# A banded attention with a feed-forward network on one core: places of all work, zeros on TensorE, and signs of the weights on other engines

## The chip, the cores and the metric

The kernel runs on one core of a Trainium2 chip. The metric is the device time of one execution in microseconds, as the median of three runs. Of the core's engines the text uses these names: PE (TensorE, matrix products), DVE (VectorE), ACT (ScalarE), POOL (GpSimd), and SP (SyncE), whose queue starts DMAs. Each engine carries out its own instructions in the order in which they stand in the program; an instruction that waits for another engine holds up what stands behind it on its own.

## The reference

```python
scores = scale * np.matmul(q, k.transpose(0, 1, 3, 2))            # B, H, S, D = 4, 8, 768, 64
is_global = pos[None, :] < int(n_global)                          # 8
is_local = (rel >= 0) & (rel < int(n_local))                      # 96
keep = is_global | is_local
dist = np.where(is_global & ~is_local, float(n_local), np.abs(rel))
scores = np.where(keep, scores - slopes[:, None, None] * dist, -1e9)
a = np.exp(scores - np.max(scores, axis=-1, keepdims=True))
x = np.matmul(a / (np.sum(a, axis=-1, keepdims=True) + 1e-09), v)
h = x.reshape(3072, 512) @ w_in                                   # w_in 512 x 2048, float64
g = np.where(h >= 1, h, np.where(h <= -1, 0.0, (h + 1) ** 2 / 4))
return g @ w_out                                                  # w_out 2048 x 512, float64
```

(Cut and joined from two functions.) The result has 3072 rows of 512 floats.

## The kernel before

**Units and chunks.** The 3072 rows are 24 units of 128 rows (batch and block of rows). Each unit's attention is done in two halves of four heads. Two units make a chunk of 256 rows for the feed-forward network, so there are 12 chunks. Units 0 to 3, the first blocks of the four batches, need only their own block of keys and are computed in float32 (functions first_*). The other 20 are computed with float16 pairs: each operand is split into a high and a low half, and three products replace one.

**A half of the attention**, for units 4 to 23: scores on PE (L742), bias and row extreme on DVE (masked, L566), the exponential on ACT (L578), high half of the probabilities on ACT (L758) and low half on DVE (L760), a DMA transpose on SP's queue (turn_p, L767, tile pt), the product with the values on PE (L785, tile av), scaling on DVE (L627, tile x), high half on ACT (L799) and low half on POOL (L801, tile xh), and a second DMA transpose on SP's queue (turn_x, L809, tile xt). In the first four units PE does the transposes (L601 for the probabilities, tile tp; L641 for the result, tile xtp), ACT copies tp to pt (L608), and DVE splits xtp (L651).

**A chunk of the feed-forward network**: eight groups of ffn1 (L870: 24 matmuls into one PSUM tile h of 128x512, for two of the 16 blocks of the hidden width), each followed by the gelu steps: ACT (L883, tile u), two on DVE (L888, L893; the second releases h), ACT (L897, tile gh), POOL (L901, tile gl). Then for each of 16 blocks and each of the chunk's two row tiles t a triple of matmuls into the tile o (ffn2, L913). ACT scales the finished o into ob (L927), and SP's queue writes it out (L928). There are two PSUM buffers for h and two for o. The transposes tp of the first units also take an h buffer.

**The weights** come as float64. In 32 pieces (n = 0 to 15 of w_in, 16 to 31 of w_out) they are loaded as pairs of 32-bit words into three raw buffers (L454, SP) and turned into float32 by DVE in three steps on 128x512: w_bits step 0 takes exponent and mantissa from the upper word (L468), step 1 the sign (L472), step 2 adds the lower word (L475) and so releases the raw buffer. Then follow w_hi (ACT, L488), w_scale (ACT, L495) and w_lo (POOL, L502). The weights are loaded a second time in 64 half pieces through the same raw buffers to be checked for their range (check_load, L529, on SP; check_reduce, L534, on DVE, two reductions to a load). At the end DVE gathers all checks, POOL reduces them over the partitions, and the verdict (badi, L297, read at L298 on SP and the other engines) decides whether a general path has to run; with these inputs it does not.

**Zeros.** warm (L434) multiplies a tile of zeros by itself, 128x128 by 128x512, into a tile named spare that nobody reads (a spare o buffer). Before, there are 8 such matmuls at the start and 3 behind each of chunk 0's eight groups, 32 in all.

**What sets the order.** Every step is entered in a list by at(time, function, arguments), with planned times from the constants at the top of the file. The list is sorted by these times, and then the table PLACE says in which order its entries are emitted. The order of each engine's instructions, and of SP's DMAs, is that of PLACE; a step that is emitted early waits on its engine.

Of the kernel before, what the change touches and what calls it, by code (L numbers as in the profile page):

```python
# [10 lines left out]
F32 = mybir.dt.float32  # L11
# [6 lines left out]
P = 128  # L18
# [38 lines left out]
XL = "p"  # L57
# [6 lines left out]
FLOAD = [-0.95, -0.52, 15.64, 24.01]  # L64
VLOAD = [-4.77, 11.54, 18.15, 28.68]
FIRST = [4.37, 7.29, 10.29, 15.54, 26.68, 37.85, 48.2, 54.41]
WARM = [(1.0, 8)]
WLOAD = [0.8, 1.0, 8.0]
WA = 3
# [3 lines left out]
TAB = -0.77  # L73
TBC = -1.99
RC = 52.97
E3 = [-19.46, -14.0, -6.17, -0.47, 3.78, 8.46, 16.26, 20.67]
PER = 47.0
SOFF = -13.94
FETCH = 16.26
CONV = 9.6  # L80
KG = 3.41
CHK = 7.39
VCONV = 10.53
VFETCH = 8.71
AVL = 14.35
GEL = [2.7, 3.48, 4.59, 5.91, 5.91]
CK0 = 199.09
CK1 = 573.64
CKL = 10.36
WO = [2.79, 3.98, 5.09]  # L90
FO = [0.26, 1.06, 2.5, 3.37, 3.48, 4.67, 5.72, 6.5, 6.59, 7.54]
UO = [0.55, 1.5, 4.0, 5.66, 6.33, 1.69, 1.96, 3.06, 3.38, 3.41]
BO = [1.94, 2.51]
SO = [0.63, 0.65, 2.38, 1.0]
WS = "d"
RO = 0.18
W0 = 6.0
PA = 2.76
WG = 3.75
PB = 2.64  # L100
NCH = NU // 2
WLAG = 5.0
PLACE = [
# [208 lines left out]
def fast_path(ctx, tc, q, k, v, nraw, nval, w_in, w_out, out, half, nm, sums, sq, su):  # L312
# [119 lines left out]
    def warm(n):  # L432
        for _ in range(n):
            nc.tensor.matmul(  # L434
                spare(0).rearrange("p (a b) -> p a b", a=4), zeros, zeros.unsqueeze(1).to_broadcast([P, 4, P]),
                start=True, stop=True,
            )

    def piece(n):
# [756 lines left out]
```

## Time and profile before

| quantity | value |
|---|---|
| median of three runs | 638.66 us (638.55 to 640.11) |
| the profiled execution's own time | 637.52 us |
| its span, first to last instruction | 635.7 us |
| mean granted clock of PE | 0.980 |
| busy PE, DVE, ACT, POOL | 607.6, 442.2, 412.1, 296.8 us |
| zero matmuls (L434) | 32 |
| DVE steps L468, L472, L475 | 32 each |

The profile describes one execution. A row of a stage gives the stage's length, each engine's busy time with its number of instructions, and the granted clock of PE as a share of full speed. A row of the waits gives the engine, the line that waited, the engine, tile and line that released it, and then the total in us, the number of waits and the longest. A row of the timeline gives start, duration, engine, line, operation and tiles, and in brackets the idle time before it with its releaser. Engines overlap, so the shares of busy time do not add up, and a wait costs time only on the engine that is the limit at that moment.

### The profile page before, as it was taken

The page shows a single profiled execution, that of the slowest core. Times are in us where ns is not written, and L with a number is a line of the kernel's source. Part 1 is how long each engine was busy: PE and PEld are TensorE (multiplying, and loading weights), DVE is VectorE, ACT ScalarE, POOL GpSimd, SP SyncE. Part 2 cuts the span into 40 slices and gives each one's busy share as a digit, 9 for nine tenths or more (in the row PEclk, how much of TensorE's full clock was granted, in tenths as well). Part 3 has the DMA queues.
Part 4 walks back from the last instruction along what each step waited for, and adds up shares of the span by engine and source line. Part 5 has one row for each costly group of instructions (what it writes and reads, how often), then busy time and mean ns, then how long its engine had stood idle before and what let it go on. Part 6 is the DMA issues. An engine that isn't in the chain of part 4 may idle for free.

```text
span 635.7 us, 14747 instructions
## 1 busy us (share of the span) xinstructions
PE 607.6 (96%) x5588; PEld 417.1 (66%) x5588; DVE 442.2 (70%) x1109; ACT 412.1 (65%) x1070; POOL 296.8 (47%) x266
## 2 busy tenths in 40 slices
PE   7888799999999999999999999999999999999996
PEld 4666575656876766767767667666666766766652
DVE  6999999977956676776776776776677686533420
ACT  4868898998867665775785775676585674432220
POOL 0336785775563543563653563463554533322210
PEclk8889899999999999999999999999999999999999
DMA  6748586578944565556555555766554643531001
GB/s 201 250 147 247 182 252 197 125 134 191 168 93 75 109 154 141 154 146 163 144 139 135 158 135 144 171 143 139 127 165 110 140 133 78 125 116 35 1 34 39
DMA packets 144084, 88.08 MB, mean 139 GB/s; under 512 B 108165, under 2 KB 124549, under 8 KB 144005
## 3 DMA queue, kind: packets, MB, share of 16 engines
q1 hardware_dynamic: 144000, 87.05, 54.1%
q8 instruction: 46, 0.75, 0.5%
q14 instruction: 34, 0.27, 0.1%
q10 hardware_dynamic: 4, 0.00, 0.0%
HBM read 54.53 MB, written 6.29 MB: 96 GB/s over the span
## 4 chain that ended last, share of the span: by engine, by line
issue 31%; POOL 26%; PE 25%; DVE 9%; ACT 5%; DMA 2%; POOLq 0%; SPq 0%; ACTq 0%; DVEq 0%
PE o L913 13%; POOL gl L901 11%; PE h L870 8%; POOL xh L801 8%; POOL kh L698 2%; POOL kr L697 2%; DVE w_f L475 2%; POOL qh L698 2%; ACT z L578 1%; POOL qr L697 1%; DMA w_raw<-in_moe_w_out_dram 1%; PE av L785 1%; POOL wol L502 1%; DVE u L893 1%; PE s L742 1%
## 5 line engine op out<-in xcount | busy, mean ns | idle before, releaser
L870 PE MATMUL h<-xt,wih 128*128 128x256 f16 x1536 | 259.7, 274 | 0.7 <-DVE u L893 0.7
L901 POOL TENSOR_TENSOR gl<-u,gh 128x512 f16<-128x512 f32 x96 | 117.8, 1227 | 214.2 <-ACT gh L897 205.2
L870 PE MATMUL h<-xt,wil 128*128 128x256 f16 x768 | 210.8, 274 | 0.0
L870 PEld LDWEIGHTS <-wih 128*128 128x128 f16 x1536 | 149.4, 99 | 32.2 <-DVE u L893 1.6
L888 DVE SCALAR_TENSOR_TENSOR h<-h,u 128x512 f32<-128x512 f32 x96 | 66.7, 695 | 116.3 <-ACT u L883 115.5
L913 PE MATMUL o<-wol,gh 128*128 128x512 f16 x384 | 145.9, 380 | 1.7 <-POOL wol L502 1.7
L913 PE MATMUL o<-woh,gh 128*128 128x512 f16 x384 | 146.4, 381 | 0.0
L913 PE MATMUL o<-woh,gl 128*128 128x512 f16 x384 | 145.8, 380 | 0.0
L883 ACT ACTIVATE u<-h,half 128x512 f32<-128x512 f32 x96 | 65.4, 682 | 87.8 <-PE h L870 87.8
L913 PEld LDWEIGHTS <-gh 128*128 128x128 f16 x768 | 71.5, 98 | 67.2 <-issue 0.5
L578 ACT ACTIVATE z<-z,nm 128x256 f32<-128x256 f32 (+1 forms) x192 | 91.8, 479 | 28.0 <-DVE nm L566 27.5
L897 ACT ACTIVATE gh<-u 128x512 f16<-128x512 f32 x96 | 59.8, 623 | 51.1 <-DVE u L893 51.1
L566 DVE CUSTOM_DVE_ANT_0 z<-s,bias 128x256 f32<-128x256 f32 (+1 forms) x192 | 67.1, 397 | 22.2 <-PE s L742 20.4
L870 PEld LDWEIGHTS <-wil 128*128 128x128 f16 x768 | 75.6, 98 | 9.1
L913 PEld LDWEIGHTS <-gl 128*128 128x128 f16 x384 | 37.7, 98 | 47.7 <-issue 2.9
L760 DVE SCALAR_TENSOR_TENSOR ph<-z,ph 128x1024 f16<-128x1024 f32 x40 | 61.6, 1540 | 9.6 <-ACT ph L758 9.4
L801 POOL TENSOR_TENSOR xh<-x,xh 128x256 f16<-128x256 f32 x40 | 62.2, 1554 | 10.4 <-ACT xh L799 8.8
L893 DVE SCALAR_TENSOR_TENSOR u<-u,h 128x512 f32<-128x512 f32 x96 | 65.4, 681 | 1.4
L534 DVE TENSOR_REDUCE sq<-c_raw 128x1 f32<-128x256 f32 x128 | 49.1, 409 | 0.0
L785 PEld LDWEIGHTS <-pt 128*128 128x128 f16 x960 | 32.8, 98 | 14.5 <-DMA pt<-ph 7.1
L758 ACT ACTIVATE ph<-z 128x1024 f16<-128x1024 f32 x40 | 41.7, 1043 | 0.1
L785 PE MATMUL av<-vh,pt 128*128 128x64 f16 x960 | 34.6, 193 | 4.5 <-DMA pt<-ph 4.3
(100 smaller groups left out, 671.8 us busy)
## 6 DMA issues: line engine op xcount, KB each, us to landing
w_raw<-in_moe_w_in_dram SPq DMA_DIRECT2D x16, 512.0 KB, 4.0
w_raw<-in_moe_w_out_dram SPq DMA_DIRECT2D x16, 512.0 KB, 3.8
c_raw<-in_moe_w_in_dram SPq DMA_DIRECT2D x32, 256.0 KB, 3.5
c_raw<-in_moe_w_out_dram SPq DMA_DIRECT2D x32, 256.0 KB, 3.3
vr<-in_v_dram SPq DMA_DIRECT2D x28, 256.0 KB, 3.9
kr<-in_k_dram SPq DMA_DIRECT2D x28, 256.0 KB, 3.6
qr<-in_q_dram SPq DMA_DIRECT2D x24, 256.0 KB, 4.3
out_dram<-ob SPq DMA_DIRECT2D x24, 256.0 KB, 2.8
```

Of the source, the lines that this page charges most:

```text
L566: nc.vector.tensor_tensor_reduce(out=p32[u, hf][:, hh, :], in0=pts[u, hf][hh // 2][:, hh % 2, 0:n], in1=bias[:, 4 * hf + hh, base : base + n],
L578: nc.scalar.activation(z, z, AF.Exp, bias=nm[:, c : c + 1], scale=-1.0, accum_out=sums[:, c : c + 1])
L760: nc.vector.scalar_tensor_tensor(phs[u, hf][:, 1, :], zf, SP_, phs[u, hf][:, 0, :], op0=ALU.mult, op1=ALU.subtract)
L785: nc.tensor.matmul(av[:, hh, :], pt[:, a, hh, kt, :], vt[:, c, h * D : (h + 1) * D], start=(n == 0), stop=(n == 5),)
L801: (nc.gpsimd if XL == "p" else nc.vector).tensor_sub(xhs[u, hf][:, 1, :], xs[u, hf], xhs[u, hf][:, 0, :])
L870: nc.tensor.matmul(hp[:, e, :], w[:, dc, f], xt[:, hf, 2 * a + j, :], start=(n == 0), stop=(n == 3 * NDC - 1),)
L883: nc.scalar.activation(us[c, g], hs[c, g], AF.Relu, bias=half, scale=2.0 / (SV * SW), accum_out=su[:, col : col + 1])
L888: nc.vector.scalar_tensor_tensor(ws[c, g], hs[c, g], 4.0 / (SV * SW), us[c, g], op0=ALU.mult, op1=ALU.max)
L893: nc.vector.scalar_tensor_tensor(dst, us[c, g], 4.0, ws[c, g], op0=ALU.min, op1=ALU.mult)
L897: nc.scalar.activation(gh, ws[c, g], AF.Copy)
L901: (nc.gpsimd if GL == "p" else nc.vector).tensor_sub(gl, ws[c, g], gt[c, g][0])
L913: nc.tensor.matmul(po, a[:, cs], w[:, f, :], start=(f == 0 and n == 0), stop=(f == NFC - 1 and n == 2))
```

## The change

Lines of the changed file are 9 to 17 higher than those of before (L472 becomes L484, L475 L487, L893 L908, L801 L816, L913 L928, and so on). The change has these parts:

- **PLACE and all planned times** are new, so every engine's order is.
- **Signs.** WS was "d" (DVE for all pieces). Now every third piece (n = 2, 5, ..., 29; ten pieces) is marked "s": DVE leaves step 1 out. ACT takes the sign of the upper word in the raw buffer, in place (L482), and POOL multiplies the finished float32 piece by it (w_sign, L494), ahead of w_hi. In these pieces POOL and not DVE is the last reader of the raw buffer.
- **XL** was "p" and is "v": the low half of x (40 subtractions of 128x256) goes from POOL to DVE (L816).
- **Zeros.** The 8 at the start are gone (WARM), two instead of three stand behind each of the eight groups (WA), and 150 entries filler() of one zero matmul each are put in the list, of which PLACE uses 95. That makes 111 zero matmuls, all ahead of the first o matmul on PE: between the score, tp, av and xtp steps of the first units and behind the first h groups, in runs of 1 to 11.
- **Check loads**: their planned times were spread from 199 to 574 us and are now from 301 to 596. The reductions of the last three check loads now follow the last gelu step on DVE.
- **The end** (TAIL): the last chunk does all 16 triples of t = 0 and then all of t = 1, in place of both in turn. The last 128 rows are scaled in two halves of 256 columns, the first by ACT and the second by DVE, which waits for ACT's write to the same tile. The first half is written out by SP's queue, the second by ACT's.
- TPO = 0 leaves the two new branches on TPO without effect.

```diff
-XL = "p"
+XL = "v"
...
-WARM = [(1.0, 8)]
+WARM = []
...
-WA = 3
+WA = 2
...
-CK0 = 199.09
-CK1 = 573.64
-CKL = 10.36
...
+CK0 = 301.36
+CK1 = 595.7
+CKL = 10.95
...
-WS = "d"
...
+WS = 'ddsddsddsddsddsddsddsddsddsddsdd'
...
 PLACE = [
-    5, 0, 1, 2, 11, 3, 6, 4, 7, 9, 12, 38, 68, 20, 8, 10, 13, 151, 14, 15, 16, 17, 18, 19, 21, 22, 25, 23, 24,
...
+    3, 0, 1, 2, 5, 7, 9, 72, 10, 4, 73, 12, 74, 75, 36, 6, 76, 230, 77, 8, 11, 14, 15, 19, 16, 17, 13, 18, 20,
...
+NFILL = 150
+TAIL = 1
+TPO = 0
...
+    def filler():
+        warm(1)
...
-            if num < NFC and num % 2:
+            if num < NFC and num % 2 and not TPO:
...
-        tp = ps_h.tile([P, 4, P], F32, tag="h", name=f"tp{u}_{hf}")
+        if TPO and u >= TPO:
+            tp = spare(1).rearrange("p (a b) -> p a b", a=4)
+        else:
+            tp = ps_h.tile([P, 4, P], F32, tag="h", name=f"tp{u}_{hf}")
...
-            nc.scalar.activation(ob[:, cs], os_[c, t][:, cs], AF.Copy, scale=1.0 / (SG * SW))
-        nc.sync.dma_start(out[r0 : r0 + P, :], ob)
+            if e:
+                nc.vector.tensor_scalar(ob[:, cs], os_[c, t][:, cs], 1.0 / (SG * SW), None, op0=ALU.mult)
+            else:
+                nc.scalar.activation(ob[:, cs], os_[c, t][:, cs], AF.Copy, scale=1.0 / (SG * SW))
+        for e in range(parts):
+            cs = slice(e * n, (e + 1) * n)
+            (nc.scalar if e else nc.sync).dma_start(out[r0 : r0 + P, cs], ob[:, cs])
...
-                at(t + 0.2, finish, c, x, 1)
+                at(t + 0.2, finish, c, x, 2 if TAIL and c + 1 == NCH and x else 1)
...
-            put_ffn2(c, (0, 1), g, t - (PER / 16 - 0.1 if g and c + 1 < NCH else 0.0))
+            if TAIL and c + 1 == NCH:
+                put_ffn2(c, (0,), g, t0 + 1.3 * g)
+                put_ffn2(c, (1,), g, t0 + 10.5 + 1.3 * g)
+            else:
+                put_ffn2(c, (0, 1), g, t - (PER / 16 - 0.1 if g and c + 1 < NCH else 0.0))
...
+    for n in range(NFILL):
+        at(12.0, filler)
```

**DVE around the gelu step of chunk 0's group 5.** The tile h0_5 is that group's PSUM tile, whose buffer the last transpose tp of the first attention takes next; w16, w17 and w18 are pieces of the weights. Before, DVE's order reads:

```order
L468 TENSOR_SCALAR w17_bits_880<-w17_raw_803 128x512
L472 SCALAR_TENSOR_TENSOR w17_bits_880<-w17_raw_803,w17_bits_880 128x512
L888 SCALAR_TENSOR_TENSOR h0_5_823<-h0_5_823,u0_5_888 128x512
L651 TENSOR_TENSOR xt1_635<-xtp3_0_883,xt1_635 128x2x128
L893 SCALAR_TENSOR_TENSOR u0_5_888<-u0_5_888,h0_5_823 128x512
L475 SCALAR_TENSOR_TENSOR w17_f32_931<-w17_raw_803,w17_bits_880 128x512
L468 TENSOR_SCALAR w18_bits_941<-w18_raw_818 128x512
L472 SCALAR_TENSOR_TENSOR w18_bits_941<-w18_raw_818,w18_bits_941 128x512
```

After:

```order
L903 SCALAR_TENSOR_TENSOR h0_5_892<-h0_5_892,u0_5_939 128x512
L666 TENSOR_TENSOR xt1_658<-xtp3_0_936,xt1_658 128x2x128
L487 SCALAR_TENSOR_TENSOR w16_f32_974<-w16_raw_829,w16_bits_920 128x512
L480 TENSOR_SCALAR w17_bits_980<-w17_raw_882 128x512
L908 SCALAR_TENSOR_TENSOR u0_5_939<-u0_5_939,h0_5_892 128x512
L487 SCALAR_TENSOR_TENSOR w17_f32_992<-w17_raw_882,w17_bits_980 128x512
L480 TENSOR_SCALAR w18_bits_1000<-w18_raw_922 128x512
L484 SCALAR_TENSOR_TENSOR w18_bits_1000<-w18_raw_922,w18_bits_1000 128x512
L487 SCALAR_TENSOR_TENSOR w18_f32_1023<-w18_raw_922,w18_bits_1000 128x512
```

Piece 17 is one of the ten: its sign step (L472 before, L484 after) no longer stands between its first and its last step, and steps of pieces 16 and 17 stand at other places around the two gelu steps.

**SP's queue at the probabilities of unit 16.** xt7 is the transposed result of units 14 and 15, pt16_0 the transposed probabilities of unit 16's first half, c13_0, c5_1 and c6_0 are check loads, ob5 the output of chunk 5. Before:

```order
L676 DMA qr18_5_5420<-in_q_dram 128x512
L529 DMA c13_0_raw_5536<-in_moe_w_in_dram 128x2x256
L809 DMA_TRANSPOSE xt7_5014<-xh15_1_5538 128x4x128
L767 DMA_TRANSPOSE pt16_0_5555<-ph16_0_5529 128x16x128
L928 DMA out_0_dram<-ob5_0_5565 128x512
L928 DMA out_0_dram<-ob5_1_5594 128x512
```

After:

```order
L541 DMA c5_1_raw_5499<-in_moe_w_in_dram 128x2x256
L948 DMA out_0_dram<-ob5_0_5505 128x512
L948 DMA out_0_dram<-ob5_1_5541 128x512
L541 DMA c6_0_raw_5572<-in_moe_w_in_dram 128x2x256
L782 DMA_TRANSPOSE pt16_0_5633<-ph16_0_5609 128x16x128
L824 DMA_TRANSPOSE xt7_5023<-xh15_1_5626 128x4x128
```

The transpose pt16_0 stood behind that of xh15_1 and stands ahead of it now; the outputs of chunk 5 went ahead of both, and the check loads are of earlier pieces. At units 18 and 20 pt still stands behind an xt.

More of the change, by code (lines that the diff above doesn't have):

```diff
@@ L62 @@
 FQ = {"k": "sync", "q": "sync", "v": "sync"}
-FLOAD = [-0.95, -0.52, 15.64, 24.01]
-VLOAD = [-4.77, 11.54, 18.15, 28.68]
-FIRST = [4.37, 7.29, 10.29, 15.54, 26.68, 37.85, 48.2, 54.41]
-WARM = [(1.0, 8)]
+FLOAD = [-1.58, 1.06, 14.93, 25.91]
+VLOAD = [-7.73, 13.43, 17.25, 33.34]
+FIRST = [4.37, 6.86, 10.29, 15.54, 27.12, 37.85, 47.39, 54.41]
+WARM = []
 WLOAD = [0.8, 1.0, 8.0]
-WA = 3
+WA = 2
 T0 = 24.5
@@ L72 @@
 GB = 5.42
[L73 to L76, printed above, removed]
+TAB = -1.61
+TBC = -0.92
+RC = 61.5
+E3 = [-19.46, -14.0, -9.93, -2.34, 1.91, 6.59, 13.05, 20.27]
 PER = 47.0
[L78 to L86, printed above, removed]
-CK0 = 199.09
-CK1 = 573.64
-CKL = 10.36
[L90 to L94, printed above, removed]
-WS = "d"
-RO = 0.18
+SOFF = -3.14
+FETCH = 17.57
+CONV = 8.38
+KG = 0.88
+CHK = 5.61
+VCONV = 8.11
+VFETCH = 5.66
+AVL = 12.92
+GEL = [2.85, 3.46, 3.99, 6.47, 7.12]
+CK0 = 301.36
+CK1 = 595.7
+CKL = 10.95
+WO = [2.78, 4.07, 6.1]
+FO = [0.65, 1.06, 2.46, 3.92, 3.63, 4.69, 5.48, 6.56, 6.65, 6.93]
+UO = [0.55, 1.5, 3.54, 5.66, 7.51, 2.65, 3.43, 3.67, 3.99, 4.75]
+BO = [1.14, 2.16]
+SO = [0.58, 0.29, 3.06, 1.83]
+WS = 'ddsddsddsddsddsddsddsddsddsddsdd'
+RO = 0.28
 W0 = 6.0
 PA = 2.76
-WG = 3.75
-PB = 2.64
+WG = 4.92
+PB = 2.85
 NCH = NU // 2
-WLAG = 5.0
+WLAG = 6.05
 PLACE = [
[139 rows of a table removed]
-]
[145 rows of a table added]
+]
+NFILL = 150
+TAIL = 1
+TPO = 0
 @with_exitstack
```

282 rows, old and new, of the table PLACE are left out of this document.

## The prediction, on record before the changed kernel ran

> **What bounds the kernel now.** I read the clock first (one core, 0.980, span 635.7 us), then busy time by stage, then TensorE's waits, then the stretch of the trace around each wait. The stages:
>
> ```profile
> 10.00:72.00 62.00, 51.52 (x343) 39.55 (x343) 57.85 (x164) 49.05 (x139) 28.88 (x26) 0.83 0.63 199
> 72.00:125.00 53.00, 50.47 (x415) 34.38 (x416) 51.44 (x102) 48.64 (x116) 37.70 (x35) 0.97 0.65 185
> 125.00:220.00 95.00, 94.55 (x1043) 66.03 (x1041) 66.73 (x167) 74.83 (x202) 54.15 (x51) 1.00 0.68 135
> 220.00:609.00 389.00, 384.69 (x3676) 265.33 (x3674) 257.37 (x631) 235.42 (x610) 174.26 (x149) 1.00 0.51 128
> 609.00:629.50 20.50, 20.46 (x95) 9.09 (x93) 2.59 (x6) 1.84 (x4) 1.53 (x2) 1.00 0.01 3
> 629.50:635.70 6.20, 0.00 (x0) 0.00 (x0) 0.00 (x0) 0.60 (x2) 0.00 (x0) 0.92 0.26 91
> ```
>
> The columns are the stretch, its length, busy PE, PEld, DVE, ACT, POOL, granted clock, DMA share, GB/s. From 72 us on PE is busy 50.47 of 53, 94.55 of 95, 384.69 of 389: nothing but PE work or PE waits can be removed there. Up to 72 us PE idles 10.48 us, although zero matmuls fill part of it, while DVE is busy 57.85 of 62: DVE sets the pace of the start. What PE waits for, over 10 to 130 us and then to the end:
>
> ```profile
> PE tp L601 <- DVE u L893: 4.4, 2, 3.9
> PE o L913 <- POOL wol L502: 1.7, 2, 1.3
> PE h L870 <- DVE u L893: 0.5, 2, 0.3
> ...
> PE av L785 <- DMA pt<-ph: 4.3, 5, 1.4
> ```
>
> The 3.9 us are the last transpose of the first attention. It waits until DVE has worked through its list to the gelu step whose PSUM buffer it takes:
>
> ```profile
> 72.26 1.09 PE L601 MATMUL tp<-ident,z 128*128 128x128 f32 x4 [3.87 <-DVE u L893]
> 73.14 0.63 PE L913 MATMUL o<-woh,gh 128*128 128x512 f16 x1
> ...
> 75.35 1.00 PE L619 MATMUL av<-vr,pt 128*128 128x64 f32 x8
> 76.19 0.38 PE L913 MATMUL o<-woh,gh 128*128 128x512 f16 x1
> 76.40 0.38 PE L913 MATMUL o<-wol,gh 128*128 128x512 f16 x1
> ...
> 76.87 0.44 PE L641 MATMUL xtp<-ident,x 128*128 128x128 f32 x2
> 77.15 0.38 PE L913 MATMUL o<-woh,gh 128*128 128x512 f16 x1
> ...
> 77.80 0.38 PE L870 MATMUL h<-xt,wih 128*128 128x256 f16 x2
> ```
>
> Before the h at 77.80 (chunk 0's eighth group) stand all of the first attention and four o triples. An o matmul takes 0.21 us at the full clock (76.19 to 76.40), so a triple 0.65.
>
> **Part by part. Signs off DVE.** What one of DVE's 128x512 steps costs there, start to start:
>
> ```profile
> 52.50 0.69 DVE L472 SCALAR_TENSOR_TENSOR w_bits<-w_raw,w_bits 128x512 int32<-128x512 int32 x1
> 53.10 0.69 DVE L468 TENSOR_SCALAR spare<-w_raw 128x512 int32<-128x512 int32 x1
> 53.69 0.68 DVE L475 SCALAR_TENSOR_TENSOR w_f<-w_raw,w_bits 128x512 int32<-128x512 int32 x1
> 54.29 0.42 DVE L627 TENSOR_TENSOR x<-av,r 128x256 f32<-128x256 f32 x1
> ```
>
> 0.60 us. Ten of 32 L472 go. In DVE's new order, six of them are missing before the release of group 0_5's buffer, else the same rows stand there: 6 x 0.60 = 3.6 us, so the transpose goes from 72.26 to about 68.65. Behind it I follow the chain in the new PE order: tp, four zeros, av, four zeros, xtp, two zeros, one o triple, group 7. The wait for pt and x now has zeros in it instead of three triples. The copy of tp to pt on ACT is this row:
>
> ```profile
> L608 ACT ACTIVATE pt<-tp 128x512 f32<-128x512 f32 x8 | 4.6, 579 | 0.0
> ```
>
> From tp to the end of xtp was 4.9 us (72.26 to 77.15), partly at half clock. Now I work out 3.6: tp 0.5 (half of 1.09, at full clock), pt 0.58 and 0.3 of hand-overs (an estimate), av 0.84 (75.35 to 76.19), x 0.42 by the L627 row and again 0.3, xtp 0.28, two zeros 0.43 (0.21 each, like an o matmul). That puts the first o near 72.3 and group 7 near 73.2 (DVE's order, 3.6 us earlier and seven L472 short by then, releases its buffer at about the same time). Three triples are then still owed, 1.95: 75.15 against 77.80, a gain of 2.6.
>
> From there to chunk 1's last group, PE is short by 45.40 - 43.13 = 2.3 us:
>
> ```profile
> 77.80:123.20 45.40, 43.13 (x373) 29.38 (x372) 44.54 (x90) 41.16 (x100) 33.11 (x31) 1.00 0.64 185
> ```
>
> DVE is at 44.54 of 45.40 there and loses the other four L472. I take 1.9 of the 2.3, as the waits named L893 and L502 both hang on DVE's list (L502 through w_f). Together 4.5; the bounds are 0 and DVE's whole relief, 10 x 0.60 = 6.0.
>
> What the ten signs cost elsewhere: one 128x512 pass on ACT and a multiply on POOL each. Neither is in the trace. The nearest rows:
>
> ```profile
> L488 ACT ACTIVATE wih<-w_f 128x512 f16<-128x512 f32 x16 | 10.0, 628 | 5.3 <-DVE w_f L475 5.1
> L502 POOL TENSOR_TENSOR wil<-w_f,wih 128x512 f16<-128x512 f32 x16 | 18.5, 1158 | 40.7 <-ACT w_f L495 40.6
> L697 POOL TENSOR_SCALAR kr<-kr 128x512 f32<-128x512 f32 x24 | 14.8, 619 | 31.9 <-ACT kh L682 31.9
> ...
> L801 POOL TENSOR_TENSOR xh<-x,xh x40: 660/1648/2517, 125.4 to 560.3; 128x256 f16<-128x256 f32 x40
> L760 DVE SCALAR_TENSOR_TENSOR ph<-z,ph x40: 1204/1336/2056, 109.1 to 549.4; 128x1024 f16<-128x1024 f32 x40
> ```
>
> (The last two rows give min/median/max in ns.)
>
> Sign: 0.63 each, 6.3 in all on an ACT with 13 us free of 62. Multiply: between 0.62 (L697, one tensor) and 1.65 (L801's median); I take 1.16 by L502, 11.6 us on a POOL busy 28.88 of 62 and 37.70 of 53. Both lie beside DVE's work, so nothing in the sum. What lies behind them: w_hi, w_scale and w_lo of that piece come 1.2 us later, and the load of piece n+3 on SP now waits for POOL, not DVE, and holds up the loads of weights, q, k and v queued behind it. If that cover goes, a piece costs up to 1.8 us (rival A).
>
> **Zeros.** 111 instead of 32, all before the first o: 79 more, 17.0 us at a third of 0.65 each, twice that at half clock. The cover is PE's waiting: 10.48 us in 10 to 72, less the 3.6 that vanish, plus what the clock gives back. Now it sits at half in five stretches (23.8 us); first and last:
>
> ```profile
> 10.40:20.60 10.20, 10.15 (x50) 7.49 (x48) 8.47 (x33) 7.99 (x30) 2.31 (x2) 0.51 0.52 168
> 71.80:75.20 3.40, 2.94 (x10) 1.68 (x11) 3.19 (x6) 3.31 (x8) 2.11 (x3) 0.53 0.40 108
> ```
>
> In the first, PE's 10.15 busy us would be about 5 at full clock, and DVE idles 1.73 that a quicker PE could return. The five hold at most 23.3 busy us, so a full clock would make some 11 of room, and the 17.0 fit, narrowly. I take 0; the bounds are 1.7 gained and rival B's loss. The Trainium skill, "TensorE: Matmul & The Clock Gate", section "What's actually happening", says that the clock is halved by default, and that a busy window of about 3.4 us releases it. The trace agrees in its steps (3.4 us, 0.51 to 0.54); by that rule the zeros pay for themselves and B cannot last, and without it the sum is the same, since I take 0.
>
> **Steady state.** Waits of av for pt are 4.3 us in five. SP's queue shows why: it issues in order, and a pt transpose stands behind one that waits for POOL.
>
> ```profile
> SPq L767 <- DVE ph L760: 115.9, 22, 9.4
> SPq L809 <- POOL xh L801: 88.8, 14, 9.7
> SPq L529 <- DVE sq L534: 13.3, 3, 4.8
> ...
> 301.00:596.00 295.00, 19.03 (x528) 18.08 (x528) 1.00 0.51 127
> ```
>
> (The last row is av's matmuls alone, 24 to a half: 22 halves in the stretch that the checks will fill.)
>
> The new order puts pt ahead of xt at some of those places (not at units 18 and 20), and the lo half of x, L801, goes from POOL at 1.65 us to DVE, which for 128x256 shows 0.42 (L627, one operand in PSUM). I let two of the five waits stay, 1.7 us, so 2.6 gained; bounds 0 and 4.3. DVE takes on 40 x 0.42 = 17 us, about 14 of them in a stage where it is busy 257.37 of 389. The 64 check loads are planned over 294 us instead of 375, one every 4.6 us instead of 5.9; more may stand ahead of a pt (rival C). I count nothing.
>
> **The tail.**
>
> ```profile
> 628.91 1.25 ACT L927 ACTIVATE ob<-o 128x512 f32<-128x512 f32 x2 [17.10 <-PE o L913]
> 629.08 0.38 PE L913 MATMUL o<-woh,gl 128*128 128x512 f16 x1
> 629.53 0.98 SPq L928 DMA_DIRECT2D out_dram<-ob  x2
> ```
>
> Last matmul ends 629.46, last eviction 630.16, end 635.7. Now the first rows are out ten us earlier, and the last come in halves: ACT about 0.40 (an estimate, somewhat over half of 1.25 / 2), then DVE (which waits for ACT's write) 0.42 as L627 for the same size, ending near 630.35, 0.2 later; but the final transfer is half as large and stands behind no other on its queue, where the two issues take 0.98. Between -0.2 and +0.8; I take +0.4. Ahead of the last rows on DVE and SP stands the verdict of the input checks (badi), which waits 7.13 us for POOL:
>
> ```profile
> 610.45 0.69 DVE L893 SCALAR_TENSOR_TENSOR u<-u,h 128x512 f32<-128x512 f32 x1
> ...
> 619.25 0.15 DVE L297 CAST badi<-anybad 128x1 int32<-128x1 f32 x1 [7.13 <-POOL anybad L295]
> ```
>
> It had 10 us to spare before 629.5. Now the reductions of three check loads, the last of them a load still to be issued, follow that last gelu step: as an estimate 6 us stand in front of it, against 1 now (610.45 + 0.69 to 619.25, less 7.13). With all 7 us earlier, badi comes near 617 and the last matmul near 622: covered by 5 us, so nothing; beyond that, each us of lateness in the checks is one of the end.
>
> **Sum.** 4.5 + 2.6 + 0.4 = 7.5 off the profiled execution's 637.52 us: 630.0. That execution is 1.1 below the median of the runs, 638.66, so 631.1 is forecast.
>
> **The rivals.**
> A, the helpers are late: ACT is busy 49.05 of 62 and every link of the first attention (exponentials, pt, hi) goes through it; ten Signs stand in that queue, and the raw buffer waits for POOL. If six signed pieces each hold DVE or the chain for the 0.60 saved, the start's gain of about 3.6 is gone: 634.7. For: ACT has only 21% free. Against: three raw buffers run ahead.
> B, slower: zeros become the bound between the first scores and the first o. If the clock stays at 0.83 in the mean, 79 zeros need 17.0 / 0.83 = 20.5 us, against 10.5 - 3.6 = 6.9 of room: 13.6 late, 644.7; it costs from the point where zeros exceed the waits by a us, and gives slower above 9.5 us. Against: a PE that full should be clocked up.
> C, SP's queue: with checks closer together the 22 halves there can each find pt late. It cancels the forecast at 7.5 / 22 = 0.34 us a half; at 0.6, 13.2 us more: 644.3. Against: 35 of 40 halves show no wait now.
> D, moving L801 does not help. L760 took 1.20 to 2.06 us here and L801 0.66 to 2.52 (its median of 1.65 is for half the elements that L502 does in 1.16), so the two hold each other up. On DVE the subtraction could stall behind POOL's 128x512 work by up to 1.16: 40 x 1.16 = 46 us of DVE, pt as late as now, and the 2.6 is not gained: 633.7. The Trainium skill, "SBUF — State Buffer", section "Who interferes with whom", says that a DVE instruction with both inputs in SBUF contends with a GpSimd instruction that reads SBUF, and that the loser of the shared pair blocks fully; the spreads agree. By it the move only exchanges who waits.
> E, nothing: the attention chain's own latency, not DVE's list, paces the start, and pt waits shift elsewhere: about 638. Against: the 3.87 us wait names DVE, which idles only 4 of the 62 us.
>
> **Chances.** Forecast 0.57 (628 to 633.5), better still 0.04, A 0.12, D 0.08, E 0.08, B 0.06, C 0.05. Range 626.0 to 636.0: the low end adds the rest of DVE's relief, pt's 1.7 and the clock's 1.7 (5 us); the high end holds A and D; E, B and C are left out, 0.19. About 0.3%, 1.9 us, is what a measurement can tell: below 636.7 faster, above 640.6 slower. Faster 0.57 + 0.04 + 0.12 + 0.08 + a little of E = 0.82; same 0.09; slower, most of B and C, 0.09.
>
> **What would show it.** Right: the last tp near 68.6, h of chunk 0's group 7 near 73, PE idle under 1 us from there to chunk 1's end, pt waits under 2 us, clock above 0.83 in 10 to 72, and 6 us from the last matmul to the end. Wrong: DVE idle before L468 on a load, PE waits named ACT or POOL's sign in the start (A); PE busy without waits and late before the first o (B); pt waits at many halves with SP's queue behind checks (C), or L801's DVE row well above 0.42 (D).

## The result, and the profile after

The changed kernel takes 629.17 us (median of 4 runs, 628.73 to 629.46) against 638.72 (638.55 to 640.11) in the same comparison: a ratio of 0.985, 95% interval 0.983 to 0.986. The profiled execution took 629.21 us, with a span of 627.4 against 635.7 and a mean granted clock of 0.999 against 0.980.

First the stages, cut as before, with the same columns (length, busy PE, PEld, DVE, ACT, POOL, clock, DMA share, GB/s):

```profile
10.00:72.00 62.00, 58.37 (x430) 41.25 (x427) 57.95 (x158) 51.87 (x142) 32.63 (x28) 1.00 0.64 201
72.00:125.00 53.00, 51.29 (x444) 34.64 (x443) 47.40 (x94) 49.39 (x116) 46.05 (x44) 1.00 0.58 175
125.00:220.00 95.00, 94.90 (x990) 65.48 (x990) 67.31 (x168) 72.80 (x195) 37.89 (x37) 1.00 0.58 124
220.00:609.00 389.00, 389.00 (x3735) 268.18 (x3730) 256.44 (x674) 242.68 (x622) 128.13 (x123) 1.00 0.54 132
```

In the start the clock row says 1.00 where it said 0.83, and PE, with its zeros, is busy for 58.37 of 62 us. (How far the row can be trusted is said under e1.) In the steady stage it is busy for all of the 389 us. Its waits up to 130 us, the rows that matter; after 130 us the view has no row at all:

```profile
PE av L634 <- ACT pt L623: 1.6, 3, 1.3
...
PE tp L616 <- DVE u L908: 1.1, 1, 1.1
PE h L885 <- DVE u L908: 0.9, 2, 0.5
...
PE o L928 <- ACT ob L945: 0.7, 1, 0.7
```

The stretch from the last tp to chunk 0's eighth group, which stood at 72.26 to 77.80 before:

```profile
69.24 0.63 PE L616 MATMUL tp<-ident,z 128*128 128x128 f32 x4 [1.08 <-DVE u L908]
...
70.88 1.10 PE L634 MATMUL av<-vr,pt 128*128 128x64 f32 x8 [0.15 <-ACT pt L623]
...
72.68 0.38 PE L656 MATMUL xtp<-ident,x 128*128 128x128 f32 x2
...
73.33 0.38 PE L928 MATMUL o<-woh,gh 128*128 128x512 f16 x1
...
73.98 0.38 PE L885 MATMUL h<-xt,wih 128*128 128x256 f16 x2
```

The tp comes 3.0 us earlier. The h at 73.98 still owes the three o triples that before stood ahead of it (1.95 us), so at equal work PE is 77.80 - 75.93 = 1.9 us ahead there. The end:

```profile
621.29 0.38 PE L928 MATMUL o<-woh,gl 128*128 128x512 f16 x1
621.76 0.38 ACT L945 ACTIVATE ob<-o 128x256 f32<-128x256 f32 x1 [9.76 <-PEq L308]
622.17 0.33 SPq L948 DMA_DIRECT2D out_dram<-ob  x1
622.18 0.42 DVE L943 TENSOR_SCALAR ob<-o 128x256 f32<-128x256 f32 x1 [10.48 <-ACT ob L945]
622.64 0.39 ACTq L948 DMA_DIRECT2D out_dram<-ob  x1
```

From the end of the last matmul (621.67) to the end of the span are 5.7 us, against 6.2 before. So the span's 8.3 us are made up of 0.5 in the tail, 4.7 in PE's waits after 130 us (4.3 and two of 0.2, all gone), and the remaining 3.1, by subtraction, in all that lies before 130 us.

### The profile page after: what moved, and what is told of

It reads as the page before. It is cut to its first block, busy times and chain, and to the rows that moved or that the text cites. A ratio compares the mean times of both kernels' runs of the same rounds, so it can differ in the third digit from the quotient of the medians.

```text
span 627.4 us, 14878 instructions
## 1 busy us (share of the span) xinstructions
PE 612.3 (98%) x5667; PEld 418.4 (67%) x5667; DVE 436.7 (70%) x1140; ACT 420.2 (67%) x1080; POOL 245.4 (39%) x236
## 5 line engine op out<-in xcount | busy, mean ns | idle before, releaser
L885 PE MATMUL h<-xt,wih 128*128 128x256 f16 x1536 | 256.4, 273 | 1.0 <-DVE u L908 0.9
L916 POOL TENSOR_TENSOR gl<-u,gh 128x512 f16<-128x512 f32 x96 | 116.1, 1209 | 285.9 <-ACT gh L912 281.8
L885 PEld LDWEIGHTS <-wih 128*128 128x128 f16 x1536 | 147.7, 98 | 32.4 <-DVE u L908 1.9
L928 PE MATMUL o<-woh,gh 128*128 128x512 f16 x384 | 145.7, 379 | 0.7 <-ACT ob L945 0.7
L928 PE MATMUL o<-wol,gh 128*128 128x512 f16 x384 | 145.5, 379 | 0.1
L928 PE MATMUL o<-woh,gl 128*128 128x512 f16 x384 | 145.5, 379 | 0.0
L928 PEld LDWEIGHTS <-gh 128*128 128x128 f16 x768 | 71.6, 98 | 68.7 <-issue 0.7
L928 PEld LDWEIGHTS <-gl 128*128 128x128 f16 x384 | 37.6, 98 | 45.7 <-issue 0.7
L908 DVE SCALAR_TENSOR_TENSOR u<-u,h 128x512 f32<-128x512 f32 x96 | 65.5, 682 | 3.5 <-DVE h L903 0.5
L775 DVE SCALAR_TENSOR_TENSOR ph<-z,ph 128x1024 f16<-128x1024 f32 x40 | 53.2, 1330 | 15.3 <-ACT ph L773 15.3
L757 PEld LDWEIGHTS <-qh 64*128 64x128 f16 x960 | 26.9, 94 | 14.9 <-issue 11.0
L590 ACT ACTIVATION_READ_ACCUMULATOR z<-z,nm 128x1 f32 x192 | 36.0, 187 | 0.0
```

The costliest lines, as they stand in the source:

```text
L590: nc.scalar.activation(z, z, AF.Exp, bias=nm[:, c : c + 1], scale=-1.0, accum_out=sums[:, c : c + 1])
L775: nc.vector.scalar_tensor_tensor(phs[u, hf][:, 1, :], zf, SP_, phs[u, hf][:, 0, :], op0=ALU.mult, op1=ALU.subtract)
L885: nc.tensor.matmul(hp[:, e, :], w[:, dc, f], xt[:, hf, 2 * a + j, :], start=(n == 0), stop=(n == 3 * NDC - 1),)
L908: nc.vector.scalar_tensor_tensor(dst, us[c, g], 4.0, ws[c, g], op0=ALU.min, op1=ALU.mult)
L916: (nc.gpsimd if GL == "p" else nc.vector).tensor_sub(gl, ws[c, g], gt[c, g][0])
L928: nc.tensor.matmul(po, a[:, cs], w[:, f, :], start=(f == 0 and n == 0), stop=(f == NFC - 1 and n == 2))
```

## The experiments

Each was timed in five rounds beside the kernel before, whose own median lay between 638.4 and 639.3 in these comparisons. That the order stays means below that the table PLACE is unchanged. A zero matmul is called a zero for short.

| label | what was changed | median us (range, runs) | ratio to before (95%) |
|---|---|---|---|
| the changed kernel | | 629.17 (628.7 to 629.5, 4) | 0.985 (0.983 to 0.986) |
| e1_no_zeros | after, no zeros | 634.90 (633.5 to 637.2, 10) | 0.994 (0.992 to 0.996) |
| e2_signs_on_dve | after, signs on DVE | 632.48 (630.9 to 633.5, 6) | 0.989 (0.987 to 0.992) |
| e7_order_and_tail_alone | after, both | 639.19 (638.2 to 640.5, 12) | 1.001 (1.000 to 1.002) |
| e3_low_x_on_pool | after, low half of x on POOL | 629.03 (628.6 to 631.9, 6) | 0.985 (0.983 to 0.988) |
| e6_before_low_x_on_dve | before, low half of x on DVE | 635.24 (633.9 to 636.5, 9) | 0.995 (0.993 to 0.997) |
| e5_before_with_zeros | before, 84 more zeros | 641.77 (638.9 to 643.9, 10) | 1.005 (1.003 to 1.007) |
| e9_half_the_zeros | after, 64 zeros | 632.05 (630.8 to 633.2, 6) | 0.990 (0.988 to 0.992) |
| e10_quarter_zeros | after, zeros a quarter as wide | 630.53 (630.4 to 633.4, 6) | 0.989 (0.986 to 0.991) |
| e4_last_rows_in_one | after, last rows in one piece | 629.60 (629.4 to 630.6, 6) | 0.985 (0.983 to 0.988) |
| e8_last_rows_side_by_side | after, a tile for each half | 629.27 (629.0 to 631.3, 5) | 0.986 (0.984 to 0.988) |
| e11_last_rows_by_columns | after, last product by columns | 627.95 (627.6 to 629.3, 5) | 0.984 (0.982 to 0.986) |
| e12_zeros_earlier | e11, three zeros moved ahead | 627.58 (627.5 to 628.6, 5) | 0.983 (0.982 to 0.985) |

My theory was the sum's: DVE's list paces the start, the zeros are covered and bring next to nothing, the steady stage gains by order and engine of the low half of x, and the tail a little. The main rival in the tests was that the clock carries the start.

**Zeros taken out.**

```diff
     def filler():
-        warm(1)
+        return
...
-        for _ in range(n):
+        for _ in range(0):
```

> The changed kernel without its 111 zero matmuls; every other instruction and its order stays. By the prediction's sum the zeros are worth nothing to 1.7 us, since DVE's list paces the start: 629.2 to 630.9. By the rival that the clock carries the start, the granted clock in 10 to 72 us falls from 1.00 back to about 0.83 and the start loses all it gained, 2.9 us or more: 632.1 and above.

634.90: 5.7 us are lost, more than three times the upper bound of my theory. The rival holds, though not by the clock row that I meant to read it from: over 10 to 72 us that row says 0.92, not 0.83. In this run from 22 to 26 us, and eight matmuls of av in the same stretch:

```profile
22.00:26.00 4.00, 3.21 (x15) 2.66 (x13) 3.93 (x9) 3.48 (x8) 1.99 (x2) 1.00 1.02 350
```

```profile
24.16 1.97 PE L634 MATMUL av<-vr,pt 128*128 128x64 f32 x8
26.65 0.48 PE L656 MATMUL xtp<-ident,x 128*128 128x128 f32 x1 [0.52 <-DVE x L642]
```

The same eight in the changed kernel:

```profile
22.98 1.00 PE L634 MATMUL av<-vr,pt 128*128 128x64 f32 x8
```

The row says 1.00, and the matmuls take twice as long. Over all av matmuls of the first attention (minimum, median and maximum in ns), e1 and then the changed kernel:

```profile
L634 PE MATMUL av<-vr,pt x64: 275/421/476, 12.5 to 74.8; 128*128 128x64 f32 x64
```

```profile
L634 PE MATMUL av<-vr,pt x64: 219/275/323, 12.8 to 71.7; 128*128 128x64 f32 x64
```

So 421 ns is the slow pace and 275 the full one (a matmul's own time overlaps with the next one's, so eight take 1.97 us against 1.00 to 1.10); in e1 they run at 421 up to 30 us, in the changed kernel never. The clock row shows half only later, at 50 to 57, 63 to 67 and 77 to 81 us. The trace's own records of the clock say why: the first one begins at 36.0 us in e1 (8.6 in the changed kernel, 6.7 in the kernel before), and where no record lies the row says 1.00. So the row and the mean clock are too high in e1, e7, e9 and e10, whose first records begin at 18 to 37 us. With PE at half pace every link of the attention chain on PE takes longer, and DVE has less to do at a time: 54.64 of the 62 us against 57.95. The last tp moved to 72.33, 3.1 us late, and group 7 runs in the last of these half-clock stretches: the next group's h stands at 83.15 in place of 78.54. These 4.6 us are the difference of the two profiled executions; e1's is 1.1 below its median.

**Signs back on DVE.**

```diff
         elif s == 1 and signed(n):
-            nc.scalar.activation(rh.bitcast(F32), rh.bitcast(F32), AF.Sign)
+            return
...
+            if signed(n):
+                nc.vector.scalar_tensor_tensor(t, rh, -0x40000000, t, op0=ALU.bitwise_and, op1=ALU.bitwise_or)
             f = f32p.tile([P, *hi.shape[1:]], I32, tag="f", name=f"w{num}_f32")
...
-        nc.gpsimd.tensor_tensor(wf[n], wf[n], wraw[n][:, :, :, 1].bitcast(F32), op=ALU.mult)
```

> The changed kernel with the ten signs back on DVE (one 128x512 step each, right ahead of the step with the lower words), without Sign on ACT and the multiply on POOL; zeros and order stay. By the prediction's sum DVE paces the start: the last tp goes 3.0 to 3.6 us later, and the time with it, 632.2 to 632.8, with up to 6 us if later pieces count too. By the clock rival, where PE's pace and not DVE's list counts, under 630.2.

632.48, 3.3 us more, as the sum's theory had it (632.2 to 632.8). The last tp in this run:

```profile
71.80 0.63 PE L617 MATMUL tp<-ident,z 128*128 128x128 f32 x4 [1.65 <-DVE u L909]
```

It is 2.6 us later for six steps of 0.60, and waits for DVE a little longer (1.65 against 1.08). The rest comes with the later pieces: at group 7 PE is 3.1 us behind. So both theories hold in part: with the zeros in place DVE's list paces the start.

**Both undone.** The edits of the two together.

> The changed kernel without zeros and with the signs on DVE: what is left is the new order, the low half of x on DVE and the tail. If zeros (5.7 us) and signs (3.3 us) each shorten a piece of their own, they add up: 638.2. If without zeros the chain through a slow TensorE paces the start, DVE has some 7 us of idle time in 10 to 65 us into which the ten steps fit: 635 to 636.

639.19: they add up, and 1.0 us more. Without zeros the signs are worth 4.3 us (639.19 to 634.90), with zeros 3.3; without signs off DVE the zeros are worth 6.7, with it 5.7. My idea that DVE's idle time at the slow clock would take the ten steps in fell. What is left (order, low half of x, tail) equals the kernel before: what the tail and the steady stage gain, the new start loses with all signs on DVE and no zeros (before has 32). In its trace PE is busy for 388.90 of the 389 us of the steady stage, but the h of group 7 stands at 82.31, at equal work (82.31 + 1.95 - 77.80) 6.5 us later than in the kernel before.

**The low half of x**, in two directions.

```diff
-XL = "v"
+XL = "p"
```

> The changed kernel with the low half of x on POOL again; order stays. If POOL's slow subtraction was what put xt in front of pt in SP's queue, some of the five waits of av return: plus 1.4 to 4.3 us, 630.6 to 633.5. If the new order of pt and xt did it alone, no wait returns: 629.2 within 0.5. By the rule that DVE and POOL block each other, DVE gets free time and L775 gets longer, without a change in time.

> The kernel before with the low half of x on DVE instead of POOL; order stays, so xt still stands in front of pt in SP's queue. If POOL's time was the cause of the late pt, most of the 4.3 us of waits go: minus 2.6 to 4.3, 634.5 to 636.1. If the place in the queue is the cause, the waits and the time stay within 0.7.

(In the second, XL goes from "p" to "v" in the kernel before.) In the new order the engine does not matter, 629.03; in the old one it is worth 4.0 us by the medians (2.8 by the two spans, 635.7 and 632.9), and PE was busy in all of the steady stage:

```profile
220.00:609.00 389.00, 389.00 (x3727) 269.19 (x3725) 267.18 (x670) 238.39 (x619) 131.94 (x120) 1.00 0.52 130
```

Either the new order or the move takes the waits for pt away; the changed kernel has both, and they don't add. (e3 keeps the zeros and the moved signs, but their last instructions lie before 110 us.) In the old order the move also costs something: between 125 and 220 us PE now waits 2.1 us for DVE's steps, against 0.4. Part of why the order suffices is in the subtraction's own time. Minimum, median and maximum in ns, first in e3 (POOL, new order), then in the changed kernel (DVE):

```profile
L816 POOL TENSOR_TENSOR xh<-x,xh x40: 662/676/1568, 123.4 to 560.2; 128x256 f16<-128x256 f32 x40
```

```profile
L816 DVE TENSOR_TENSOR xh<-x,xh x40: 405/417/1381, 124.4 to 560.2; 128x256 f16<-128x256 f32 x40
...
L775 DVE SCALAR_TENSOR_TENSOR ph<-z,ph x40: 1205/1226/2194, 109.1 to 548.4; 128x1024 f16<-128x1024 f32 x40
```

The same instruction on POOL had a median of 1648 in the old order and has 676 in the new one. In the old order 30 of the 40 took more than 0.9 us, and 29 of these 30 overlap a step L760 of DVE; of the ten short ones one does. In e3 13 take more than 0.9 us. This agrees with the Trainium skill's rule ("SBUF — State Buffer", section "Who interferes with whom") that a DVE instruction with two inputs in SBUF contends with a GpSimd instruction that reads SBUF. L760, too, went from a median of 1336 to 1226 (L775), but not on account of the subtraction: in e6, with the subtraction on DVE, it is still 1336 (24 of 40 above 1.3 us, all beside other POOL work).

Where the five waits were tells the two effects of the order apart. They stood at pt of units 10, 16, 18, 20 and 22, each directly behind the xt of the half before. At units 18 and 20 pt is still behind an xt, but the subtraction ahead of it is short now. At unit 18, in the kernel before and in e3:

```profile
414.81 2.51 POOL L801 TENSOR_TENSOR xh<-x,xh 128x256 f16<-128x256 f32 x1
```

```profile
417.98 0.67 POOL L816 TENSOR_TENSOR xh<-x,xh 128x256 f16<-128x256 f32 x1 [2.58 <-ACT xh L814]
```

At unit 10 it is the other way round: the subtraction still takes 1.57 us in e3, but pt stands ahead of that xt. At units 16 and 22 both changed.

**Zeros in the old order.** Four ahead of the scores, of tp and of av of the first seven halves:

```diff
+        if (u, hf) < (3, 1):
+            warm(4)
         whole(u, hf)
```

> The kernel before with 4 more zero matmuls ahead of the scores, of tp and of av of the first seven first halves, 84 in all, nothing else changed. If the granted clock is what the zeros bring and the start of before loses by it, the clock in 10 to 72 us rises from 0.83 to near 1.00 and the time falls by 1.7 to 4 us (636.7 to 634.5). If DVE's list sets the start of before (it idles 4.15 of 62 us), the clock rises and the time falls by less than 1. By rival B of the prediction the zeros come late: 640 and more.

641.77, 2.6 us slower. The clock went up, and it did not help. Stage, and the last tp:

```profile
10.00:72.00 62.00, 57.64 (x425) 40.42 (x422) 53.64 (x159) 45.98 (x128) 26.05 (x23) 1.00 0.58 184
```

```profile
76.22 1.08 PE L605 MATMUL tp<-ident,z 128*128 128x128 f32 x4 [5.54 <-DVE u L899]
```

PE is as full as in the changed kernel (57.64), but DVE was busy for 53.64 us in place of 57.85, and comes to that gelu step 4.0 us later. The zeros stood ahead of PE's steps whether PE had to wait there or not. From 10 to 30 us PE was busy for 19.95 of 20 us (17.64 before) and DVE for only 16.10 (18.01 before), and the av of the fourth half started at 32.79 us in place of 29.73, though at full pace. So the zeros held up what DVE needed next. Rival B, in milder form, is what zeros do when they are not put into the gaps.

**Fewer zeros, and narrower ones.**

```diff
     def filler():
-        warm(1)
+        fills.append(0)
+        warm(len(fills) % 2)
```

> The changed kernel with every second one of the 95 placed zero matmuls left out, 64 in all instead of 111. If the zeros act by keeping TensorE's clock up and all are needed, part of the 5.7 us comes back: the first attention's matmuls go to half pace in places, 631 to 633. If half of them keep the clock up, the rest only stood in front of useful work (PE is busy without a gap from 22 to 58 us): 627.5 to 629. If zeros act by their count alone, half the loss: 632.0.

```diff
-                spare(0).rearrange("p (a b) -> p a b", a=4), zeros, zeros.unsqueeze(1).to_broadcast([P, 4, P]),
+                spare(0)[:, 0:P], zeros, zeros,
```

> The changed kernel with all 111 zero matmuls in their places, but 128 columns wide instead of 512, so a quarter of the busy time each. If it is TensorE's busy share that holds the clock, 6 us of zeros instead of 24 don't hold it, and the first attention's matmuls run at half pace: 633 to 635. If a matmul now and then is enough, the time stays or falls by up to 1: 628.2 to 629.4.

632.05 and 630.53 (of the second four runs near 630.5 and two, the profiled one among them, at 632.7 and 633.4, so its trace shows the longer kind). Both lose. The first lies where "all are needed" and where "half the loss" by the count alone had put it; the second lies in neither of its two ranges. In e9 the av matmuls are at full pace from 20 us on, in e10 from 25 us, where the changed kernel is there before 13, and both fall back later. Two rows of e10:

```profile
19.73 1.92 PE L634 MATMUL av<-vr,pt 128*128 128x64 f32 x8
...
61.38 1.97 PE L634 MATMUL av<-vr,pt 128*128 128x64 f32 x8 [0.26 <-ACT pt L623]
```

In both, the records of the clock fall to half at 59 us. The 3.41 us ahead of that, in e10 and then in the changed kernel, whose clock stays up:

```profile
55.86:59.27 3.41, 0.00 (x0) 0.00 (x0) 3.27 (x9) 1.63 (x3) 1.61 (x2) 1.00 0.84 287
```

```profile
55.86:59.27 3.41, 3.34 (x20) 1.77 (x19) 3.33 (x8) 1.73 (x5) 1.46 (x2) 1.00 0.91 298
```

PE was busy for 0 us, 0.78 in e9 and 3.34 in the changed kernel. In the kernel before, each of the five half-clock stretches follows 3.41 us in which PE was busy for 0.23 to 2.20 us. So it is how busy PE is in such a stretch, and not the total number of zeros, that the clock follows: e10 has all 111. No threshold is shown, nor that busy time alone explains the loss, since e10 with a quarter of it mostly loses less than e9 with half. The zeros of the changed kernel are not too many: without half of them half of their gain is lost.

**The tail.**

```diff
-                at(t + 0.2, finish, c, x, 2 if TAIL and c + 1 == NCH and x else 1)
+                at(t + 0.2, finish, c, x, 1)
```

> The changed kernel with the last 128 rows scaled by ACT alone and sent in one transfer; the last chunk still does t = 0 ahead of t = 1. If the halves give the tail its gain (0.8 us by the traces), the end falls back by 0.4 to 0.8: 629.6 to 630.0. If it is that the first rows left ten us earlier, nothing changes: 629.2 within 0.2.

629.60, 0.4 more. The end of that run:

```profile
621.13 0.38 PE L928 MATMUL o<-woh,gl 128*128 128x512 f16 x1
621.61 0.60 ACT L945 ACTIVATE ob<-o 128x512 f32<-128x512 f32 x1 [9.76 <-PE o L928]
622.23 0.33 SPq L948 DMA_DIRECT2D out_dram<-ob  x1
```

The span ended at 627.9, 6.4 us after the last matmul's end, against 5.7 with halves. The halves carry the gain, not the early rows (6.2 before, when both row tiles ended together), and not by the scaling: the one pass of ACT ends earlier (622.21) than the two halves (622.60). What is left is the last transfer: it is half as large, and it goes out by another engine's queue; this run does not part the two.

```diff
-        ob = f32p.tile([P, DM], F32, tag="f", name=f"ob{c}_{t}")
+        obs = [f32p.tile([P, n], F32, tag="f", name=f"ob{c}_{t}_{e}") for e in range(parts)]
```

> The changed kernel with a tile of its own for each half of the last rows, so that DVE does not wait for ACT's write and both scale side by side. If the serial scaling is on the path to the end, the last scaling ends 0.40 us earlier and the time with it: 628.8. If the transfers or what follows them set the end, within 0.15 of the changed kernel.

629.27, unchanged; but the experiment did not do what it was for. DVE still started only when ACT had ended (621.84 us, behind ACT's 0.38 us from 621.42), presumably because both read the same PSUM tile, so it tells nothing of scaling side by side. Then the product itself by columns, each half with a PSUM tile and a tile of its own (shown in part):

```diff
+            for x in range(2):
+                for y in (range(NFC) if x and f == NFC - 1 else () if x else (f,)):
...
+                        nc.tensor.matmul(
+                            os_[c, t][x], a[:, cs], w[:, y, x * CH : (x + 1) * CH],
+                            start=(y == 0 and n == 0), stop=(y == NFC - 1 and n == 2),
+                        )
```

> The changed kernel with the last 128 rows' product done by columns: all matmuls for the first 256 columns, then all for the other 256, into two PSUM tiles. DVE scales and SP sends the first half under the second half's matmuls; after the last matmul there is only ACT's half of 0.38 us. If the scaling after the last matmul is on the path to the end, it is 0.42 us shorter: 628.7. If what follows (transfer, end of program) sets the end by itself, within 0.15 of the changed kernel; if 256-column matmuls cost more than half of 512-column ones, slower.

627.95, 1.2 less than the changed kernel, where I had expected 0.4. Its end:

```profile
621.96 0.27 PE L930 MATMUL o<-woh,gl 128*128 128x256 f16 x1
622.32 0.38 ACT L958 ACTIVATE ob<-o 128x256 f32<-128x256 f32 x1 [9.88 <-PE o L930]
622.74 0.38 ACTq L961 DMA_DIRECT2D out_dram<-ob  x1
```

The span ends at 626.3, 4.1 us after the last matmul's end. From the issue of the last DMA to the end are 3.6 us, against 4.8 in the changed kernel, where the other half's transfer of the same size is issued 0.47 us ahead of it on another engine's queue. That is 1.2 of the 1.6 us by which the tail is shorter than the changed kernel's 5.7; the rest is the scaling, which I had expected to be all. The Trainium skill, "DMA: Bandwidth & Descriptors", section "Issuing engines are not separate DMA queues", says that such DMAs run on the same 16 engines and interleave; the runs agree with it. Last, on top of e11, three zeros into the wait ahead of pps_n, with the first three fillers left out for them (not shown):

```diff
         nc.vector.memset(zeros, 0.0)
+        warm(3)
```

> The kernel of the last rows by columns, with three of the first six zero matmuls moved ahead, from behind the second start-up matmul (pps_n) into the 1.3 us in which TensorE waits for it. If the clock rises once TensorE has been busy for some 3 to 5 us, it is at full pace 1.3 us earlier and the first scores, at 7.44 us in the changed kernel, start 1.2 us earlier: 626.8 to 627.7 against 627.95. If DVE's list sets the pace from the first half on, the lead is lost by the last tp and the time stays at 627.95 within 0.3.

627.58: in the first range and 0.07 below the second, and the runs of e11 and e12 overlap, so the time does not decide. The first scores start at 7.22 us in place of 7.52, a lead of 0.3 and not 1.2, because they now wait 0.92 for a load. The last tp, in e11 and in e12:

```profile
69.66 0.63 PE L616 MATMUL tp<-ident,z 128*128 128x128 f32 x4 [1.08 <-DVE u L908]
```

```profile
69.62 0.63 PE L620 MATMUL tp<-ident,z 128*128 128x128 f32 x4 [1.08 <-DVE u L912]
```

The small lead is lost on the way, as DVE's list would have it. e11 and e12 are the fastest versions, with ratios of 0.984 and 0.983 to the kernel before.

## Why the prediction was right, and where not

**The time**, 631.1 in a range of 626.0 to 636.0, was 1.9 us too high, and the direction right. The terms of the sum were 4.5, 2.6 and 0.4; the trace has 3.1, 4.7 and 0.5. That the total came so near is in part luck: the first term was 1.4 too high, the second 2.1 too low (1.7 on the waits for pt alone), and what the start gained holds a gain of the zeros, which I had put at nothing.

**Signs.** Right in mechanism: the last tp follows DVE's list, and undoing the ten steps costs 3.3 us. The size was off where I let each missing step count in full: 69.24 and not 68.65 for tp, and the undoing moves it by 2.6, not 3.6. The chain from tp to group 7 took 4.7 us against the 4.55 worked out. Of the 2.3 us of waits up to chunk 1's end I let 0.4 stay; between 72 and 125 us 1.7 stayed (53.00 - 51.29), 0.9 of them on the gelu step and 0.7 on a wait that before did not have, o for ACT's scaling of the chunk ahead. So the sign "PE idle under 1 us from there to chunk 1's end" did not come.

**Zeros.** This step failed: "I take 0; the bounds are 1.7 gained and rival B's loss." They are worth 5.7 us. I had judged by how little DVE idled in the old half-clock stretches, that is, in an order that was built around them; in the new order the slow PE holds up the start, with the signs off DVE (5.7 us, e1) and on it (6.7, e7). The end of the sum came out near because the base had 32 zeros and a clock of 0.83 already, and because the terms that I did count lean on the full clock: tp at 0.5, av at 0.84. They contain the zeros' work without naming it. That the 17 us fit into the gaps was right on the whole: PE is busy for 58.37 of 62 us, and taking half of the zeros out (e9) gained nothing. That no single step is late by them is not shown.

**Steady stage.** Right that the waits for pt go, and too cautious: all five went. Wrong on why: I gave the order and the engine a part each, and either alone takes away all of it. The order works by the place of pt in SP's queue at unit 10, and by POOL's shorter subtraction (0.68 us in the median in place of 1.65) at units 18 and 20, where pt still stands behind an xt.

**The rivals.** A did not come: ACT 51.87 of 62, and SP's waits for POOL's sign are there without reaching PE. What was not in the trace, Sign and the multiply, took 0.67 and 1.29 us (medians), against 0.63 and 1.16 taken. B did not come here but does with zeros put elsewhere (e5). C did not come, though its cause did:

```profile
SPq L541 <- DVE sq L546: 56.6, 19, 9.7
```

SP's queue waits 56.6 us for check reductions, against 13.3, and no av waits for it. D fell: the subtraction takes 0.417 us on DVE, and e6 shows that the move does help. The contention that it named is real for L801, but not the cause of L760's time. E fell: the last tp came earlier with DVE's list, and no wait for pt is left.

**The tail.** Forecast 0.4, measured 0.5, by the last transfer as put down (its size or its queue); the verdict of the checks was ready at 611.5, ten us ahead of the last matmul, earlier than the 617 that I had estimated.

## What to carry to other kernels

Zero matmuls in the waits of TensorE can be worth much (5.7 us here), since they keep the clock up for the short chain of small matmuls that follows; zeros ahead of work that is ready made the other order 2.6 us slower. So first find the waits, then fill them, and judge by the durations of useful matmuls and not by the clock row. When two edits aim at the same wait, undo each alone in the new kernel and do each alone in the old one: only so does it show that one would have been enough. At the end of a program, look at what is transferred last: in e11 half the bytes, with nothing else under way, were worth 1.2 us, and the shorter scaling 0.4.

## What the runs showed of the hardware that was not expected

- The clock row can read 1.00 while f32 matmuls of 128x64 take 421 ns and not 275 (e1, 12 to 30 us): the trace holds no record of the clock up to 36.0 us.
- The clock falls to half although PE had work in the 3.41 us ahead: with 0.78 us of it busy in e9, and with up to 2.20 in the kernel before.
- A subtraction of 128x256 on POOL takes 0.68 or 1.65 us in the median, in two versions of the program (e3 and the kernel before); nothing in the instruction itself differs, but 29 of the 30 long ones overlap a step of DVE with two inputs in SBUF.
- The last transfer of 128x256 takes 3.6 us from its issue to the end of the program alone (e11) and 4.8 beside another one (the changed kernel), each in one profiled execution.
